# A planned attention and gated-convolution kernel: another plan for the same work, and the causal mask issued per head

## The chip, the cores and the metric

The kernel runs on one core of a Trainium2 chip. The metric is the device time of one execution in microseconds (us); lower is better. The inputs lie in HBM as float32, and the output goes back there as float32.

## The reference

```python
# q, k, v: [8, 8, 576, 64]   s: [8, 8, 576]   (batch, head, position, head width)
scores = q @ k.T / 8
cum    = cumsum(max(s, 0))                       # along the positions
scores = where(causal, -1e9, scores + min(-(cum_i - cum_j), 0))
attn   = softmax(scores)                         # [576, 576] per head
x      = (attn @ v) laid out as [8, 576, 512]    # heads side by side
# 5-tap causal convolution along the positions, per channel
gate   = sigmoid(sum_k conv_w[k] * shift(x, 4 - k))
out    = (gate * (x @ w_val)) @ w_out            # [8, 576, 512]
```

## The kernel before, in words

The eight batches are worked one after another, but heavily overlapped. Each batch has four head pairs; a head pair is numbered `n` = 4 x batch + pair, so `n` runs from 0 to 31. The decay `exp(cum)` is folded into v, so that a score needs only a plain `exp`. The steps of a head pair, with their lines in the profile:

- **Load and cast.** SyncE (SP) hands all transfers to its DMA queue. Q and K of a batch come in float32 and are cast to bf16 (L524; the last 64 positions, the "tail", L695 for batch 0 and L721 after it). For batch 0 this is cut into eight pieces (`first`, two per head pair) that DVE, ACT or POOL casts; from batch 1 on, POOL casts it in two large pieces.
- **Transpose.** TensorE (PE) transposes them into PSUM (`qk_T` L563, `tail_T` L552), ACT or DVE copies that to SBUF (`qk_evac` L567, `tail_evac` L555).
- **Scores.** `scores` (L572) has three steps of 1,024 columns (two heads x 512) in a pair of PSUM banks each; `exps` (L598, always on ACT) writes `P`. The diagonal blocks of both heads all lie in step 0, and POOL's `mask` (L604) zeroes what lies above the diagonal, over 2 x 512 columns, with one `affine_select`. The last 64 queries go the same way in `scores4`, `exp4` (L584) and `mask4` (L609), once per batch (in batch 0 per head pair).
- **Weighted sum.** `vprime` (L534, POOL; two of batch 0 on DVE) scales v; `av` (L619) multiplies P with it, `recip` (L624) and `norm` (L629) on DVE divide by the sum, `x_T` (L637) transposes back, `x_evac` (L641, DVE or ACT) copies to SBUF.
- **Gate.** Four `tap` steps per head pair, each on DVE (one instruction, L653 or for tap 1 L655) or on POOL (two instructions: L650 `tmp`, L651 `gp`); each tap reads the result of the tap before. Then `tanh` on ACT (L659).
- **Output.** `val` (L666) and `glu` (L672, DVE) per channel block, `outp` (L678), `out_evac` (L683, ACT or DVE), `store` (L686, SP).

The order of all this is no hand-written list. The program records every step as a task with an engine, an assumed duration, a due time, what it depends on and which buffers and PSUM banks it takes. `Plan.run` then plays these tasks through in a model and emits them in the order in which the model started them; each engine works through its own list strictly in that order. The due times are in the dictionary `DUE`, the choice of engine of the steps that have one is in `CHOICE` (a digit per step), `STAY` is the reluctance to turn PE between two kinds of work (scores, which use 64 rows of the array, and all the rest), and `BEHIND` is how far the DMA queue may be behind in the model before SP has to wait. All these are numbers fixed before the build; on the chip only the order and the engines are left of them.

```python
t = add("ACT", 0.905, n + 0.3 * i, lambda n=n, i=i: exps(n, i), [t], give=[("pair", ("s", n, i))])
es += [t] if i else [add("POOL", 0.75, n + due("mask"), lambda n=n: mask(n), [t])]
```

Of the kernel before, what the change touches and what calls it, by code (L numbers as in the profile page):

```python
# [14 lines left out]
ALU = mybir.AluOpType  # L15
# [190 lines left out]
def pcol(kb, qb):  # L206
    if kb == qb:
        return kb * 128
    if qb == 4:
# [13 lines left out]

DUE = dict(w=-179.07, lwv=6.9, lwo=25.99, cwv=119.71, cwo=21.81, av=-67.91, norm=-106.36, xt=-83.29,
           xe=-39.43, tap=73.53, dtap=-12.21, tanh=-21.14, val=7.28, dval=1.38, out=12.56, dout=0.92,
           oute=44.7, qt=-5.37, qe=224.11, tt=0.85, te=-141.54, s4=-66.86, vp=-112.81, cast=107.85,
           lqk=56.02, mask=-117.33, lv=13.25, av_e=68.91, av_l=-46.36, cast_e=-153.69, cast_l=-53.98,
           dout_e=-12.2, dout_l=-66.84, dtap_e=-10.04, dtap_l=-64.5, dval_e=14.84, dval_l=-0.73,  # L230
           lqk_e=-53.46, lqk_l=16.33, lv_e=84.68, lv_l=-81.16, mask_e=2.46, mask_l=30.46, norm_e=62.66,
           norm_l=45.33, out_e=82.66, out_l=-73.32, oute_e=83.06, oute_l=-53.09, qe_e=-68.49, qe_l=46.96,
           qt_e=-24.08, qt_l=3.94, s4_e=27.55, s4_l=-86.7, tanh_e=20.1, tanh_l=94.17, tap_e=-15.62,
           tap_l=-2.33, te_e=-55.59, te_l=-34.48, tt_e=-48.5, tt_l=-36.85, val_e=-96.42, val_l=2.31,
           vp_e=-46.58, vp_l=160.49, xe_e=32.24, xe_l=-1.61, xt_e=14.3, xt_l=-78.88, sd=-18.85, lcw=-44.05,
           cvt=23.68, rat=-67.55, lt0=-98.57, tailc0=29.75, lq0=-12.67, lq0d=2.97, cast0=-5.61,
           cast0d=127.18, lv0=-3.45, lv0d=2.76, vp0=32.35, vp0d=-5.83, tt0=62.96, te0=134.74, qt0=19.06,
           qe0=-26.31, q0d=25.23)


def due_of(b, name):
# [2 lines left out]

STAY = (1.35, 151.9)

BEHIND = 11.48

CHOICE = dict(tailc="2",
              vp0="1100",
              cast="00112001",
              wts="00",
              te="00000100",
              qe="01110110001000001001110000100100",
              xe="01111000001011110000000100100111",
              tap="00000000100001000000000100010000010000001100000000000010100000001000011000000010000100010000010010000110000100000100010010110000",
              oute="0010011001000000110010100000000010001100")


class Plan:
# [12 lines left out]
    def add(self, eng, us, key, emit, deps=(), take=(), give=(), mode="N", pick=None):  # L275
        alts = list(zip(eng, us)) if pick else [(eng, us)]
        eng, us = alts[int(CHOICE[pick[0]][pick[1]]) if pick else 0]
        if pick:
            emit = partial(emit, eng)
        t = dict(pick=pick, alts=alts, eng=eng, us=us, key=key, emit=emit, deps=[d for d in deps if d is not None], take=take,  # L280
                 give=give, mode=mode, n=len(self.tasks), done=None)
        self.tasks.append(t)
        return t
# [101 lines left out]
def main_path(ctx, tc, q, k, v, s, moe_w_val, moe_conv_w, moe_w_out, out, okcnt):  # L385
# [5 lines left out]
    nc = tc.nc  # L391
# [4 lines left out]
    add, slot = plan.add, plan.slot  # L396
# [49 lines left out]
    w = one.tile([128, NKB, 64], FP32, name="w")  # L446
# [29 lines left out]

    t = add("DVE", 0.65, DUE["sd"], relu, [t_s])
    t = add("DVE", 1.3, DUE["sd"], total, [t])
    t = add("DVE", 0.75, DUE["sd"], centre, [t])
    t = add("PE", 1.2, DUE["w"], decay_T, [t], take=[("bank", "w")])  # L480
# [5 lines left out]
    for m, (nm, src, dst, sc) in enumerate((("wv", moe_w_val, wv, 1.0), ("wo", moe_w_out, wo, 0.5))):  # L486
# [3 lines left out]
        t = add("SP", 2.8, DUE["l" + nm], load, take=[("qkf", nm)])  # L490
# [9 lines left out]
    t = add("SP", 0.3, DUE["lcw"], lambda: nc.sync.dma_start(out=cw, in_=moe_conv_w))  # L500
    t = add("PE", 0.3, DUE["cvt"], conv_T, [t], take=[("bank", "cw")])
# [97 lines left out]
                             func=AF.Exp, scale=0.125)  # L599


    def mask(n):
        d = slot["Pt", n][:, :, 0:512].rearrange("k h (g q) -> k h g q", g=4)
        nc.gpsimd.affine_select(out=d, in_=d, pattern=[[0, 2], [0, 4], [1, 128]], compare_op=ALU.is_ge, fill=0.0, base=0,  # L604
                                channel_multiplier=-1)

    def mask4(b, ps_):
# [80 lines left out]
    for b in range(B):  # L688
        n0 = 4 * b
        due = partial(due_of, b)  # L690
        old = lambda name: [T.get((name, b - 2, i)) for i in range(4)]

        if b == 0:
# [3 lines left out]
            for p in range(4):  # L697
                for wh in range(2):
# [3 lines left out]
                    t = add("SP", 0.82, DUE["lq0"] + DUE["lq0d"] * p + wh * 0.01, ld)  # L702
                    T["cast", 0, wh, p] = add(("DVE", "ACT", "POOL"), (0.32, 0.5, 0.8), DUE["cast0"] + p * DUE["cast0d"], lambda e, p=p, wh=wh: cast_qk(
                        copy[e], 0, wh, HP[p], slot["f", 0, wh, p]), [t], pick=("cast", 2 * p + wh))
                t = add("SP", 1.45, DUE["lv0"] + DUE["lv0d"] * p, lambda p=p: load_v_pair(p))
                T["vp", 0, p] = add(("DVE", "POOL"), (0.85, 1.25), DUE["vp0"] + p * DUE["vp0d"], lambda e, p=p: vprime(
                    nc.vector if e == "DVE" else nc.gpsimd, 0, p), [t, t_w], pick=("vp0", p))
        else:
            fs = []
            for wh in range(2):  # L710
# [3 lines left out]
                t = add("SP", 3.25, n0 + due("lqk"), ld, take=[("qkf", (b, wh))])  # L714
# [5 lines left out]
            t = add("SP", 1.45, n0 + due("lqk") + 0.5, lambda b=b: load_tail(b), [T.get(("tailc", b - 2))])  # L720
# [4 lines left out]
            for p in range(4):  # L725
# [4 lines left out]
        t = T["tt", b] = add("PE", 0.25, n0 + due("tt") if b else DUE["tt0"], lambda b=b: tail_T(b), [t_tail] + old_s,  # L730
                             take=[("bank", ("tt", b))])
        t_te = add(("ACT", "DVE"), (0.49, 0.6), n0 + due("te") if b else DUE["te0"], lambda e, b=b: tail_evac(e, b), [t],
                   give=[("bank", ("tt", b))], pick=("te", b))
        for p in range(4):
            t = T["qt", b, p] = add("PE", 0.45, n0 + p + due("qt") if b else DUE["qt0"] + p * DUE["q0d"], lambda b=b, p=p: qk_T(b, p),
                                    [T["cast", b, 0, p], T["cast", b, 1, p]] + old_s, take=[("bank", ("qt", b, p))])
# [4 lines left out]
        for ps_ in ([[p] for p in range(4)] if b == 0 else [[0, 1, 2, 3]]):  # L741
            n = len(ps_)
            t = T["s4", b, ps_[-1]] = add(
                "PE", 0.06 + 0.035 * n, n0 + ps_[0] + due("s4"), lambda b=b, ps_=ps_: scores4(b, ps_),
                [t_te] + [T["qe", b, p] for p in ps_] + [T.get(("av", b - 2, p)) for p in range(4)],
                take=[("pair", ("s4", b, ps_[0]))], mode="R")
            t = add("ACT", 0.08 + 0.1 * n, n0 + ps_[0] + due("s4"), lambda b=b, ps_=ps_: exp4(b, ps_), [t],
                    give=[("pair", ("s4", b, ps_[0]))])
            t = add("POOL", 0.15 + 0.11 * n, n0 + ps_[0] + due("mask"), lambda b=b, ps_=ps_: mask4(b, ps_), [t])
            for p in ps_:  # L750
                e4[p] = t
        for p in range(4):
            n = n0 + p
            es = []
            for i in range(3):
                take = [("pair", ("s", n, i))] + ([("P", n)] if i == 0 else [])
                t = T["s", n, i] = add("PE", 0.26, n + 0.3 * i, lambda n=n, i=i: scores(n, i),
                                       [T["qe", b, p], t_te if i else None, T.get(("s", n, i - 1)), T.get(("s", n - 1, 2))],
                                       take=take, mode="R")
                t = add("ACT", 0.905, n + 0.3 * i, lambda n=n, i=i: exps(n, i), [t], give=[("pair", ("s", n, i))])  # L760
                es += [t] if i else [add("POOL", 0.75, n + due("mask"), lambda n=n: mask(n), [t])]
            for hh in range(2):
                t = T["av", b, p] = add("PE", 0.45, n + due("av") + 0.1 * hh, lambda n=n, hh=hh: av(n, hh),
                                        [t] if hh else es + [e4[p], T["vp", b, p], T.get(("xt", n - 8))],
                                        take=[] if hh else [("pair", ("av", n))], give=[("P", n)] if hh else [])
            t = add("DVE", 0.13, n + due("norm"), lambda n=n: recip(n), [t])
            t = T["norm", n] = add("DVE", 0.74, n + due("norm"), lambda n=n: norm(n), [t], give=[("pair", ("av", n))])
            t = T["xt", n] = add("PE", 0.3, n + due("xt"), lambda n=n: x_T(n),
                                 [t] + [T.get(("val", n0 - 8 + c, hf)) for c in range(4) for hf in range(2)]
                                 + [T.get(("tap1", n - 8))], take=[("bank", ("x", n)), ("gp", n)])  # L770
            t = T["xe", n] = add(("DVE", "ACT"), (0.37, 0.65), n + due("xe"), lambda e, n=n: x_evac(e, n), [t],
                                 pick=("xe", n))
            for sh in range(1, 5):
                t = add(("DVE", "POOL"), (0.73, 2.25), n + due("tap") + sh * due("dtap"), lambda e, n=n, sh=sh: tap(e, n, sh),
                        [t, t_cw], give=[("bank", ("x", n))] if sh == 4 else [], pick=("tap", 4 * n + sh - 1))
                if sh == 1:
                    T["tap1", n] = t
            T["th", n] = [add("ACT", 0.59, n + due("tanh"), lambda n=n: tanh(n), [t], take=[("th", n)],
                              give=[("gp", n)])]

        for c in range(4):
            n = n0 + c
# [8 lines left out]
        for i in range(NKB):  # L791
# [4 lines left out]
            t = add(("ACT", "DVE"), (0.49, 0.6), n0 + due("oute") + due("dout") * i, lambda e, b=b, i=i: out_evac(e, b, i),  # L796
                    [t], take=[("ot", (b, i))], give=[("bank", ("o", b, i))], pick=("oute", 5 * b + i))
# [82 lines left out]
```

## Time and profile before

| what | value |
|---|---|
| median of 3 runs | 216.9 us (216.85 to 217.32) |
| the profiled execution, its own time | 216.85 us |
| its span in the profile | 215.1 us |
| busy: PE, DVE, ACT, POOL | 176.6, 172.8, 166.0, 177.0 us |
| time with which the chain of waits charges POOL | 31% of the span |
| granted TensorE clock, mean | 0.965 |

The span runs from the first to the last recorded event of the core; the 1.75 us between it and the execution's time lie around it. "Busy" is the summed time of an engine's instructions. All four computing engines are within 11 us of each other, so a share of the whole span doesn't say which of them holds the others up: that has to be read stretch by stretch.

### The profile page before, as it was taken

The numbers are of one execution on the slowest core, as the hardware profiler recorded it, in microseconds if no ns is written. First come the engines' busy times: TensorE is split into PE (matmuls) and PEld (weight loads), VectorE is DVE, ScalarE is ACT, GpSimd is POOL, SyncE is SP. The second block draws the span as 40 slices with busy tenths as digits, with TensorE's granted clock in tenths as the row PEclk, the third lists the DMA queues.
The fourth block names the chain that finished last, engine by engine and source line by source line (L and its number), as shares of the span: only waits on it lengthen the run. The fifth ranks groups of instructions, "written<-read, shape, count | busy, mean of one in ns | idle before, by whom it ended". The sixth has DMA issues, their size and how long they took to land.

```text
span 215.1 us, 5995 instructions
## 1 busy us (share of the span) xinstructions
PE 176.6 (82%) x2394; PEld 120.2 (56%) x2411; DVE 172.8 (80%) x295; ACT 166.0 (77%) x214; POOL 177.0 (82%) x161
## 2 busy tenths in 40 slices
PE   0488866788997997699998898789996998998980
PEld 0355755357655756367745674657664665664630
DVE  0496798696999895788989898899979687889930
ACT  2579269967798789979899999588996899965430
POOL 5069576799989999999999999999996899985400
PEclk9999979699999999979999999999999799999998
DMA  4998999999999599928994911186057122114333
GB/s 103 318 215 253 388 187 255 334 229 283 204 364 334 172 222 369 370 91 160 306 392 159 213 28 50 52 169 150 0 126 199 38 83 78 49 52 168 129 122 113
DMA packets 69230, 40.48 MB, mean 188 GB/s; under 512 B 47109, under 2 KB 63493, under 8 KB 69194
## 3 DMA queue, kind: packets, MB, share of 16 engines
q1 hardware_dynamic: 69194, 40.01, 67.8%
q8 instruction: 21, 0.34, 0.7%
q14 instruction: 15, 0.12, 0.2%
HBM read 30.57 MB, written 9.44 MB: 186 GB/s over the span
## 4 chain that ended last, share of the span: by engine, by line
POOL 31%; PE 20%; DVE 13%; issue 13%; ACT 12%; SPq 4%; DMA 3%; POOLq 0%; DVEq 0%; ACTq 0%
POOL Vp L534 8%; POOL gp L651 7%; POOL tmp L650 7%; ACT P L598 6%; PE banks L619 6%; PE banks L678 5%; PE banks L666 5%; POOL P L604 5%; DVE gp L653 3%; DVE xn L629 3%; DMA first<-in_k_dram 2%; DVE glu L672 2%; PE banks L572 2%; PE banks L563 2%; SPq L540 2%
## 5 line engine op out<-in xcount | busy, mean ns | idle before, releaser
L598 ACT ACTIVATE P<-banks 128x1024 bf16<-128x1024 f32 x96 | 95.1, 1037 | 10.1 <-PE banks L572 9.6
L653 DVE SCALAR_TENSOR_TENSOR gp<-banks,ratio,gp 128x572 f32<-128x572 bf16 (+2 forms) x77 | 61.3, 804 | 6.2 <-POOL gp L651 5.5
L572 PE MATMUL banks<-QKT 64*128 64x128 bf16 (+4 forms) x576 | 39.1, 251 | 10.4 <-ACT P L598 4.2
L619 PE MATMUL banks<-Vp,P 128*128 128x65 bf16 x960 | 37.9, 200 | 5.9 <-POOL P L604 2.8
L666 PE MATMUL banks<-xT,wv 128*128 128x288 bf16 x256 | 40.5, 296 | 1.9 <-DVE gp L653 1.2
L619 PEld LDWEIGHTS <-P 128*128 128x128 bf16 x960 | 35.7, 102 | 11.4 <-issue 3.7
L678 PE MATMUL banks<-wo,glu 128*128 128x512 bf16 x143 | 38.4, 380 | 3.0 <-DVE glu L672 0.9
L534 POOL TENSOR_TENSOR Vp<-vst,w 128x650 bf16<-128x650 f32 x30 | 39.0, 1321 | 1.8 <-ACT w L481 1.8
L604 POOL TENSOR_SCALAR_AFFINE_SELECT P<-P 128x1024 bf16<-128x1024 bf16 x32 | 35.1, 1099 | 5.1 <-ACT P L598 4.8
L572 PEld LDWEIGHTS <-QKT 64*128 64x128 bf16 x576 | 18.9, 97 | 27.2 <-issue 20.1
L650 POOL TENSOR_TENSOR tmp<-xT,ratio 128x574 f32<-128x574 bf16 (+3 forms) x25 | 28.6, 1146 | 2.8 <-ACT xT L641 2.2
L666 PEld LDWEIGHTS <-wv 128*128 128x128 bf16 x256 | 23.3, 100 | 13.3 <-issue 6.8
L672 DVE SCALAR_TENSOR_TENSOR glu<-th,banks 128x288 bf16<-128x288 f32 x64 | 27.7, 446 | 3.1 <-PE banks L666 2.8
L651 POOL TENSOR_TENSOR gp<-tmp,gp 128x574 f32<-128x574 f32 (+2 forms) x19 | 26.8, 1413 | 3.7 <-DVE gp L653 2.4
L659 ACT ACTIVATE th<-gp,halfw 128x576 f32<-128x576 f32 x32 | 24.9, 785 | 5.3 <-DVE gp L653 5.3
L629 DVE TENSOR_TENSOR xn<-banks,recs 128x640 bf16<-128x640 f32 x32 | 26.2, 820 | 0.5
L683 ACT COPY ot<-banks 128x512 f32<-128x512 f32 (+1 forms) x29 | 17.1, 599 | 9.7 <-PE banks L678 7.2
L678 PEld LDWEIGHTS <-glu 128*128 128x128 bf16 x160 | 14.3, 98 | 17.2 <-issue 4.7
L567 ACT COPY QKT<-banks 128x1024 bf16<-128x1024 bf16 x20 | 20.0, 1024 | 4.8 <-PE banks L563 4.8
L655 DVE SCALAR_TENSOR_TENSOR gp<-xT,ratio,banks 128x576 f32<-128x576 bf16 x26 | 21.0, 808 | 0.8 <-ACT xT L641 0.3
L637 PE MATMUL banks<-ident,xn 128*128 128x128 bf16 x160 | 14.1, 219 | 3.2 <-DVE xn L629 2.0
L567 DVE COPY QKT<-banks 128x1024 bf16<-128x1024 bf16 x12 | 14.4, 1216 | 2.6 <-PE banks L563 2.6
(63 smaller groups left out, 176.3 us busy)
## 6 DMA issues: line engine op xcount, KB each, us to landing
out_dram<-ot SPq DMA_DIRECT2D x32, 256.0 KB, 2.9
qkf<-in_q_dram SPq DMA_DIRECT2D x7, 1024.0 KB, 7.3
qkf<-in_k_dram SPq DMA_DIRECT2D x7, 1024.0 KB, 8.5
vst<-in_v_dram SPq DMA_DIRECT2D x28, 256.0 KB, 4.8
vst<-in_v_dram SPq DMA_DIRECT2D x15, 128.0 KB, 5.0
tail<-in_q_dram SPq DMA_DIRECT2D x8, 128.0 KB, 7.9
tail<-in_k_dram SPq DMA_DIRECT2D x8, 128.0 KB, 7.0
first<-in_q_dram SPq DMA_DIRECT2D x4, 256.0 KB, 4.7
```

Of the source, the lines that this page charges most:

```text
L534: eng.tensor_tensor(Vps[b % 2][:, :, h], vst[:, :, h], w[:, :, b * 8 + 2 * p:b * 8 + 2 * p + 2].unsqueeze(3).to_broadcast([128, NKB, 2, 65 ...
L567: copy[e](QKTs[b % 2][:, :, p, 0:512].rearrange("d w (x j) -> d w x j", j=4), slot["qt", b, p].rearrange("d w (j x) -> d w x j", j=4))
L572: nc.tensor.matmul(ps[:, hh, c0:c0 + nq], QKTs[b % 2][r, 1, p, k0:k0 + 128], QKTs[b % 2][r, 0, p, q0:q0 + nq], **kw)
L598: nc.scalar.activation(out=slot["Pt", n][:, :, step * 512:(step + 1) * 512], in_=slot["s", n, step], func=AF.Exp, scale=0.125)
L604: nc.gpsimd.affine_select(out=d, in_=d, pattern=[[0, 2], [0, 4], [1, 128]], compare_op=ALU.is_ge, fill=0.0, base=0, channel_multiplier=-1)
L619: nc.tensor.matmul(ps[:, hh, qb * 65:qb * 65 + 65], lhsT, Vps[b % 2][:, kb, 2 * p + hh, :], start=(kb == 0), stop=(kb == qb))
L629: nc.vector.tensor_tensor(xns[b % 2][:, :, p * 128:(p + 1) * 128].rearrange("t g (h d) -> t h g d", h=2), pv[:, :, :, 0:64], recs[:, n].un ...
L650: nc.gpsimd.tensor_tensor(tmp[:, o:S], xs[:, 2 - sh + o:2 - sh + S], r.to_broadcast([128, S - o]), ALU.mult)
L651: nc.gpsimd.tensor_tensor(gp[:, o:S], tmp[:, o:S], gp[:, o:S] if o else xs[:, 2:], ALU.add)
L653: nc.vector.scalar_tensor_tensor(gp[:, o:S], slot["x", n][:, 0:S - o], r, gp[:, o:S], ALU.mult, ALU.add)
L666: nc.tensor.matmul(ps, wv[:, dc, c * 128:(c + 1) * 128], xTs[b % 2][:, dc, 2 + o:290 + o], start=(dc == 0), stop=(dc == 3))
L678: nc.tensor.matmul(ps, glus[b % 2][:, c, WIN[i]:WIN[i] + 128], wo[:, c, :], start=(c == 0), stop=(c == 3))
```

## The change

The tasks, their buffers and their arithmetic stay; the numbers of the plan are others, and one task is cut in two.

- `mask` is issued once per head (two `affine_select` of 512 columns) in place of once per head pair (one of 1,024). The plan now counts 2 x 0.6 us for it, before 0.75 us.
- `DUE`, `STAY` (1.35, 151.9 to 2.87, 127.12) and `BEHIND` (11.48 to 10.11) have other values, which puts the tasks of every engine in another order.
- `CHOICE` moves steps between engines. Counted over all batches, before to after: taps on POOL 25 to 19 (tap 1: 6 to 4; tap 2: 8 to 3; tap 3: 5 to 2; tap 4: 6 to 10); `qk_evac` on DVE 12 to 11; `x_evac` on DVE 18 to 19; `out_evac` on DVE 11 to 9; `tail_evac` on DVE 1 to 0; casts of batch 0 on DVE, ACT, POOL 4, 3, 1 to 3, 4, 1; the tail cast of batch 0 from POOL to DVE.

The built order, read from the two programs: PE turns between scores and other work 116 times before and 106 times after; a tap follows a tap of the same head pair on the other engine (DVE and POOL) 30 times before and 20 after. In the first batch SP hands out s one pair of pieces earlier, and the first two v transfers before the last Q and K pieces:

```
SP before: tail, conv_w, q0 k0, q1 k1, s, q2 k2, q3 k3, v0, v1, v2, v3, batch 1 ...
SP after:  tail, conv_w, q0 k0, s, q1 k1, q2, v0, k2, v1, q3 k3, v2, v3, batch 1 ...
ACT before: tail_evac 0, cast q1, qk_evac 0, cast k1, exp4 0, exps 0 (three), cast k3, w, exp4 1, ...
ACT after:  tail_evac 0, cast k0, cast q1, cast q2, exp4 0, exps 0 (three), w, exp4 1, ...
DVE before: conv ratios, cast q0, cast k0, relu, cumsum, cast k2, centre, qk_evac 1, qk_evac 2, cast q3, ...
DVE after:  tail cast, conv ratios, cast q0, relu, qk_evac 0, cumsum, centre, qk_evac 1, cast k2, cast q3, qk_evac 2, ...
PE end before: ... x_T 31, outp 6 (two), val 28, outp 6 (three), count, val 29, 31, 30, outp 7 (five)
PE end after:  ... x_T 31, outp 6 (five), val 28, 29, count, val 31, 30, outp 7 (five)
```

In the last batch POOL has the taps 30/1, 30/3 and 30/4 before, 30/1 and 30/2 after.

```diff
-           ... sd=-18.85, lcw=-44.05,
-           cvt=23.68, rat=-67.55, lt0=-98.57, tailc0=29.75, lq0=-12.67, lq0d=2.97, cast0=-5.61,
-           cast0d=127.18, lv0=-3.45, lv0d=2.76, vp0=32.35, vp0d=-5.83, tt0=62.96, te0=134.74, qt0=19.06,
-           qe0=-26.31, q0d=25.23)
+           ... sd=-15.74, lcw=-22.57,
+           cvt=-10.73, rat=-74.99, lt0=-86.14, tailc0=47.9, lq0=-10.92, lq0d=2.77, cast0=12.28,
+           cast0d=98.87, lv0=-5.37, lv0d=1.44, vp0=70.86, vp0d=-8.38, tt0=49.65, te0=84.67, qt0=29.8,
+           qe0=0.26, q0d=39.82)
...
-STAY = (1.35, 151.9)
-BEHIND = 11.48
+STAY = (2.87, 127.12)
+BEHIND = 10.11
...
-CHOICE = dict(tailc="2",
+CHOICE = dict(tailc="0",
               vp0="1100",
-              cast="00112001",
+              cast="01121001",
               wts="00",
-              te="00000100",
-              qe="01110110001000001001110000100100",
-              xe="01111000001011110000000100100111",
-              tap="00000000100001000000000100010000010000001100000000000010100000001000011000000010000100010000010010000110000100000100010010110000",
-              oute="0010011001000000110010100000000010001100")
+              te="00000000",
+              qe="11100110000000001110110000100000",
+              xe="01111000001010110000000010110011",
+              tap="00010000100000000001000100010000000100000000100000000000100000000001000000000101000000100000000100010000000001100001000011000000",
+              oute="0000001000001000010101100000010000001100")
...
-    def mask(n):
-        d = slot["Pt", n][:, :, 0:512].rearrange("k h (g q) -> k h g q", g=4)
-        nc.gpsimd.affine_select(out=d, in_=d, pattern=[[0, 2], [0, 4], [1, 128]], compare_op=ALU.is_ge, fill=0.0, base=0,
+    def mask(n, hh):
+        d = slot["Pt", n][:, hh, 0:512].rearrange("k (g q) -> k g q", g=4)
+        nc.gpsimd.affine_select(out=d, in_=d, pattern=[[0, 4], [1, 128]], compare_op=ALU.is_ge, fill=0.0, base=0,
                                 channel_multiplier=-1)
...
-                es += [t] if i else [add("POOL", 0.75, n + due("mask"), lambda n=n: mask(n), [t])]
+                es += [t] if i else [add("POOL", 0.6, n + due("mask") + 0.01 * hh, lambda n=n, hh=hh: mask(n, hh), [t])
+                                     for hh in range(2)]
```

All other entries of `DUE` (due times of the later batches) change as well.

More of the change, by code (lines that the diff above doesn't have):

```diff
@@ L222 @@
 NEG = -30000.0
[L226 to L235, printed above, removed]
-           cvt=23.68, rat=-67.55, lt0=-98.57, tailc0=29.75, lq0=-12.67, lq0d=2.97, cast0=-5.61,
-           cast0d=127.18, lv0=-3.45, lv0d=2.76, vp0=32.35, vp0d=-5.83, tt0=62.96, te0=134.74, qt0=19.06,
-           qe0=-26.31, q0d=25.23)
@@ new lines @@
+DUE = dict(w=-146.29, lwv=18.35, lwo=25.55, cwv=66.29, cwo=20.07, av=-62.19, norm=-66.39, xt=-62.08,
+           xe=-40.28, tap=59.48, dtap=-11.23, tanh=-60.59, val=7.98, dval=1.19, out=13.07, dout=0.7,
+           oute=35.59, qt=-4.95, qe=212.03, tt=1.64, te=-107.11, s4=-34.19, vp=-83.31, cast=103.59,
+           lqk=30.41, mask=-106.85, lv=19.28, av_e=59.94, av_l=-18.88, cast_e=-150.32, cast_l=-44.48,
+           dout_e=-18.55, dout_l=-90.65, dtap_e=-17.77, dtap_l=-16.53, dval_e=23.29, dval_l=2.97,
+           lqk_e=-22.85, lqk_l=14.05, lv_e=56.66, lv_l=-121.96, mask_e=19.74, mask_l=17.23, norm_e=50.91,
+           norm_l=8.42, out_e=93.56, out_l=-44.02, oute_e=121.54, oute_l=-99.96, qe_e=-63.7, qe_l=55.19,
+           qt_e=-69.75, qt_l=4.1, s4_e=-5.62, s4_l=-62.13, tanh_e=26.16, tanh_l=103.46, tap_e=-8.19,
+           tap_l=19.63, te_e=-35.56, te_l=-17.97, tt_e=-12.58, tt_l=-2.26, val_e=-88.07, val_l=-6.49,
+           vp_e=-38.23, vp_l=139.1, xe_e=-4.6, xe_l=10.49, xt_e=-36.76, xt_l=-24.73, sd=-15.74, lcw=-22.57,
+           cvt=-10.73, rat=-74.99, lt0=-86.14, tailc0=47.9, lq0=-10.92, lq0d=2.77, cast0=12.28,
+           cast0d=98.87, lv0=-5.37, lv0d=1.44, vp0=70.86, vp0d=-8.38, tt0=49.65, te0=84.67, qt0=29.8,
+           qe0=0.26, q0d=39.82)
```

## The prediction, made before the changed kernel ran

> **What bounds the kernel now.** I began with the top of the page, whose busy times hardly tell the engines apart, so I read the slices next, then the chain of waits.
>
> ```profile
> span 215.1 us, 5995 instructions
> PE 176.6 (82%) x2394; PEld 120.2 (56%) x2411; DVE 172.8 (80%) x295; ACT 166.0 (77%) x214; POOL 177.0 (82%) x161
> ...
> POOL 5069576799989999999999999999996899985400
> ...
> POOL 31%; PE 20%; DVE 13%; issue 13%; ACT 12%; SPq 4%; DMA 3%; POOLq 0%; DVEq 0%; ACTq 0%
> ```
>
> POOL is idle early and late and solid from about the eighth slice on; the chain charges it most, and DMA 3%. The view by windows says where (columns: length, then busy us of PE, PEld, DVE, ACT, POOL with instruction counts, the clock, the DMA share, GB/s):
>
> ```profile
> 0.00:40.00 40.00, 24.84 (x333) 18.61 (x334) 27.67 (x43) 25.93 (x36) 24.12 (x35) 0.95 0.94 248
> 40.00:145.00 105.00, 92.90 (x1350) 63.86 (x1358) 90.39 (x158) 90.83 (x114) 102.72 (x85) 0.97 0.82 224
> 145.00:180.00 35.00, 31.51 (x441) 21.02 (x445) 30.82 (x54) 30.78 (x40) 31.50 (x27) 0.95 0.38 97
> 180.00:195.00 15.00, 14.39 (x205) 9.80 (x205) 12.71 (x25) 11.85 (x17) 14.08 (x13) 1.00 0.19 72
> 195.00:215.10 20.10, 13.00 (x76) 6.87 (x73) 11.20 (x21) 6.58 (x11) 4.55 (x4) 0.97 0.38 129
> ```
>
> From 40 to 145 us POOL works 102.72 of 105 us (98%) and the others 86 to 88%: there POOL is the bound. From 145 to 180 it stands at 90%, like PE; after 180 PE leads (14.39 of 15), and after 195 POOL has almost nothing. So what POOL saves counts fully between 40 and 145, in part up to 195, and hardly elsewhere.
>
> **POOL, the mask in two.** The timeline of POOL gives the price from start to start, which is what a full queue pays (columns: start, busy, engine, line):
>
> ```profile
> 112.23 0.66 POOL L609 TENSOR_SCALAR_AFFINE_SELECT P<-P 128x512 bf16<-128x512 bf16 x1
> 112.86 2.52 POOL L534 TENSOR_TENSOR Vp<-vst,w 128x650 bf16<-128x650 f32 x2
> 115.34 1.10 POOL L604 TENSOR_SCALAR_AFFINE_SELECT P<-P 128x1024 bf16<-128x1024 bf16 x1
> 116.40 1.28 POOL L534 TENSOR_TENSOR Vp<-vst,w 128x650 bf16<-128x650 f32 x1
> ```
>
> A select of 1,024 columns keeps the queue for 116.40 - 115.34 = 1.06 us, one of 512 (`mask4`, the size of the new half) for 0.63. Two halves cost 1.26, so the split adds about 0.2 us per head pair, 32 x 0.2 = 6.4 us in all. Lower end: if a half cost just half of 1.06, nothing is added; upper end by busy times, 2 x 0.66 - 1.10 = 0.22, 7.0 us. I take 6.4, since the 512-column row has the very size. No gain is in it: the data is the same.
>
> [...]
>
> **POOL, the taps.** The groups:
>
> ```profile
> L650 POOL TENSOR_TENSOR tmp<-xT,ratio 128x574 f32<-128x574 bf16 (+3 forms) x25 | 28.6, 1146 | 2.8 <-ACT xT L641 2.2
> L651 POOL TENSOR_TENSOR gp<-tmp,gp 128x574 f32<-128x574 f32 (+2 forms) x19 | 26.8, 1413 | 3.7 <-DVE gp L653 2.4
> L653 DVE SCALAR_TENSOR_TENSOR gp<-banks,ratio,gp 128x572 f32<-128x572 bf16 (+2 forms) x77 | 61.3, 804 | 6.2 <-POOL gp L651 5.5
> ```
>
> A tap on POOL is 1.15 + 1.41 = 2.56 us (a tap 1, whose second instruction is a shape of its own at 1.20, is 2.35), on DVE 0.80. 25 to 19: two tap 1 (4.7) and four others net (10.2) leave, -14.9 us on POOL. The tail cast of batch 0 leaves too (0.6). POOL's sum: 177.0 - 14.9 - 0.6 + 6.4 = 167.9 us.
>
> Where these fall, by the built order of POOL:
> - From the mask of head pair 5 (starts at 42.72) to that of 23 (145.17), the stretch in which POOL is the bound: 18 masks cost 18 x 0.2 = 3.6 more, one `mask4` moves out (-0.63), taps go from 11 to 9 (-2.35 - 2.56 = -4.9). Net **-1.9 us**, nearly all on the path. Bounds: -5.5 (halves that add nothing) to -1.6 (by 0.22).
> - From 23 to 31 (187.61): masks +1.6, `mask4` +0.63, taps 8 to 6, -4.9: net -2.7 us. PE and POOL share this stretch, so half passes: **-1.3** (0 to -2.7).
> - Behind mask 31: 4 taps to 2, -5.1 us, beside PE, which sets the end; **0** here.
> - Ahead of mask 5 the sums are equal within 0.3 us.
>
> **DVE and ACT.** DVE: taps +6 x 0.80 = 4.8; one `qk_evac` less, -1.2; `x_evac` +0.45; two `out_evac`, -1.4; tail copy -0.4; one cast -0.6; the tail cast +0.5: +2.2 us, 172.8 to 175.0. ACT: +1.0 - 0.65 + 2 x 0.6 + 0.6 + 0.6 = +2.8, 166.0 to 168.8. In 40:145 DVE has 14.6 us free and ACT 14.2, so these are covered; without that cover they would cost up to 2.8 us. PE's instructions are the same.
>
> **Waits between engines.** 30 to 20 changes of engine within a chain of taps, where DVE waited 5.5 us for POOL in seven places (L653's row); DVE isn't the bound there, so 0, with -1.5 as the far end. PE turns 116 to 106 times:
>
> ```profile
> PEld L572 <- issue: 20.1, 52, 1.1
> ```
>
> The weight load of the scores stands idle 0.39 us at 52 of the turns. Ten fewer are 3.9 us of PE, which PE at 88% needn't pass on: 0, with -3.9 as the far end. The order of SP's transfers: the same bytes and issues; in the 40:145 window the chain is on POOL, not on a landing, so 0; what goes late first is the v load, which waits for the last `vprime` of the batch before, and that comes no later.
>
> **The start.** `qk_evac 0` moves from ACT to DVE, behind `relu`, which waits for s. Before, s went out at 4.89 and relu began at 10.01, 5.1 us later. It now goes out two issues (0.5 us each) earlier, so relu starts near 9.0, the copy (1.22 us) ends near 10.7 where ACT's ended at 10.10; `cast q2` (landed at 10.64) now also stands in front of ACT's first exp. First exp +0.6 us. Against that ACT stood idle 3.27 + 0.78 us at 21.7 to 26.1 for the scores of head pair 3, whose `qk_evac` now is on ACT, behind `cast k3` and `x_evac 1`. Between -1 and +1; I take **+0.3**.
>
> **The end.** Behind norm 31, DVE gets a tap and a glu more and an `out_evac` less (0.80 + 0.45 - 0.68 = +0.57), but no longer waits for POOL's taps 30/3 and 30/4 (there 0.28 and 0.43 us). PE runs all of batch 6's output ahead of `val 28`. -1 to +1; **0**.
>
> **Sum.** -1.9 - 1.3 + 0.3 = -2.9 us at full passing. I let four fifths of POOL's 3.2 pass, because the next engines are at 88% and each waits for others: -2.6 + 0.3 = -2.3. The profiled execution took 216.85 us (span 215.1 and 1.75 around it; the median of the runs is 216.9, the same to 0.05): 216.85 - 2.3 = **214.5 us**.
>
> **Rivals.**
> 1. *Nothing passes.* POOL's 1.9 us turn into waits for PE, DVE and ACT, which are all within 12% of full in the same window. For it: the four sums become 176.6, 175.0, 168.8 and 167.9, and PE's is unchanged. Against it: no engine but POOL gets over 88.5% in 40:145. Time 216.5 to 217.3.
> 2. *Slower: the last tap on POOL blocks ACT.* Tap 4 goes from 6 to 10 on POOL, and tap 4 is what `tanh` waits for; ACT works in order, so a late tap 4 holds the exps queued behind `tanh`, with them the scores' PSUM banks, PE and then POOL's own masks. A tap 4 on POOL is 2.56 - 0.80 = 1.76 us longer. All ten exposed: 17.6 us. It decides above 2.6 / 10 = 0.26 us each; with a third exposed (0.6 us each) it is 6 us, less 2.3: 220.5 us. Against it: with six such taps before, ACT's waits name DVE alone,
>
> ```profile
> ACT th L659 <- DVE gp L653: 5.3, 6, 2.1
> ```
>
> and in the new order two to six exps stand between the mask ahead of the tap and the `tanh`. For it: tap 0/4 now stands ahead of the tail cast of batch 1 and has just two. A milder form gives 217.5 to 219.
> 3. *Much faster.* PE was the second bound throughout, and the ten turns (3.9 us) come on top: 216.85 - 2.3 - 3.9 = 210.7 us.
> 4. *The transfers matter after all*, as the name of the change says. Waits for a DMA outside the first 12 us are small (POOL's tail casts, 1.1 us in two), so it gives 215.5 to 217 and joins rival 1.
>
> **How the numbers follow.** A difference below 0.2% (0.4 us) can't be told from none here. Forecast, 212 to 216.4: 0.50. Much faster: 0.08. Nothing passes: 0.10, of which 0.07 lies within 0.2% and the rest on both sides. Slower by the tap or another wait of a new order: 0.32. Faster 0.59, same 0.07, slower 0.34. Range 211.2 to 219.5: below it lies about half of the "much faster", above it a quarter of the slower cases. The forecast's own range is 212 to 216.4.
>
> **What would show it.** In the changed profile: 64 selects at L604 at about 0.66 us; POOL near 168 us busy; masks 5 to 23 in about 100 us in place of 102.45; POOL still the busiest engine in that stretch. Wrong if the halves cost 0.55 or less (then POOL gains 6 us more), if ACT waits over 5 us for `gp` of POOL at `tanh` (rival 2), if the first exp comes over 1 us later and mask 5 with it, or if POOL falls under 93% between masks 5 and 23 with no gain (rival 1).

## The result, and the profile after

The changed kernel takes 211.51 us in the median (211.02 to 211.99, 4 runs) against 217.0 us before: ratio 0.9745, 95% interval 0.9716 to 0.9774, so about 5.5 us faster. It was measured twice more beside the kernel before: 0.9737 (0.9684 to 0.9791) and 0.9736 (0.9695 to 0.9776). The profiled execution took 211.99 us, its span is 210.3 us, 4.8 us less than before. The forecast was 2.3 us: the right way, less than half of the size.

The top of the page after, POOL's slices and the chain of waits:

```profile
span 210.3 us, 6022 instructions
PE 173.6 (83%) x2390; PEld 119.9 (57%) x2411; DVE 173.8 (83%) x298; ACT 168.7 (80%) x218; POOL 165.2 (79%) x180
...
POOL 4059589579999999999999999997979969838000
...
PE 30%; DVE 25%; POOL 14%; ACT 12%; issue 10%; DMA 3%; SPq 2%; ACTq 0%; DVEq 0%; POOLq 0%
```

POOL has 11.8 us less to do and is charged with 14% of the chain in place of 31%; PE and DVE now carry it. The stretches, cut at the masks of head pairs 5, 23 and 31 and at the end of the last `norm`, show where the time came from. First before, then after (columns: stretch, length, busy us of PE, PEld, DVE, ACT, POOL with counts, clock, DMA share, GB/s):

```profile
0.00:42.72 42.72, 27.16 (x345) 19.90 (x346) 28.87 (x44) 28.65 (x40) 26.76 (x37) 0.92 0.95 256
42.72:145.17 102.45, 90.62 (x1340) 62.62 (x1348) 89.36 (x155) 88.28 (x112) 100.08 (x83) 0.98 0.82 220
145.17:187.61 42.44, 38.73 (x545) 25.66 (x551) 36.60 (x64) 37.78 (x48) 39.03 (x33) 0.96 0.34 92
187.61:194.25 6.64, 6.36 (x94) 4.59 (x92) 6.01 (x12) 4.60 (x7) 5.88 (x6) 1.00 0.17 61
194.25:215.10 20.85, 13.75 (x81) 7.38 (x80) 11.95 (x23) 6.66 (x11) 5.22 (x5) 0.97 0.38 131
```

```profile
0.00:43.53 43.53, 27.71 (x359) 20.99 (x360) 30.65 (x50) 29.01 (x40) 25.99 (x41) 0.96 0.96 252
43.53:141.96 98.43, 87.68 (x1333) 61.91 (x1343) 86.55 (x149) 89.37 (x112) 96.92 (x96) 0.97 0.84 226
141.96:184.39 42.43, 40.05 (x543) 26.12 (x551) 40.09 (x73) 39.36 (x52) 36.03 (x39) 1.00 0.34 98
184.39:188.56 4.17, 4.12 (x78) 3.38 (x78) 4.00 (x8) 4.10 (x6) 1.23 (x2) 1.00 0.32 118
188.56:210.30 21.74, 14.01 (x82) 7.54 (x82) 12.54 (x24) 6.86 (x11) 5.04 (x4) 0.93 0.35 120
```

The start costs 0.8 us more, the stretch from mask 5 to mask 23 gives 4.0, the next one nothing, the rest 1.6 (6.64 + 20.85 - 4.17 - 21.74). In the third stretch the length is the same, but PE does 1.3 and DVE 3.5 us more in it: work that then is missing behind mask 31. The granted clock is no explanation: its mean is 0.965 before and 0.969 after, and in the stretch that gave most it is 0.98 before and 0.97 after.

The price of the mask in two, in POOL's timeline of the changed kernel:

```profile
63.69 1.24 POOL L604 TENSOR_SCALAR_AFFINE_SELECT P<-P 128x512 bf16<-128x512 bf16 x2
64.89 1.15 POOL L650 TENSOR_TENSOR tmp<-xT,ratio 128x572 f32<-128x572 bf16 x1
```

A pair of halves keeps the queue 64.89 - 63.69 = 1.20 us, 0.14 more than the single select's 1.06; the prediction had taken 0.2 from the `mask4` row.

### The profile page after: what moved, and what is told of

Same layout as the page of the kernel before. It is cut to its first block, busy times and chain, and to the rows that moved or that the text cites. A ratio compares the mean times of both kernels' runs of the same rounds, so it can differ in the third digit from the quotient of the medians.

```text
span 210.3 us, 6022 instructions
## 1 busy us (share of the span) xinstructions
PE 173.6 (83%) x2390; PEld 119.9 (57%) x2411; DVE 173.8 (83%) x298; ACT 168.7 (80%) x218; POOL 165.2 (79%) x180
## 4 chain that ended last, share of the span: by engine, by line
PE 30%; DVE 25%; POOL 14%; ACT 12%; issue 10%; DMA 3%; SPq 2%; ACTq 0%; DVEq 0%; POOLq 0%
DVE gp L653 8%; PE banks L666 8%; PE banks L678 6%; PE banks L619 6%; PE banks L572 5%; ACT P L598 5%; DVE glu L672 4%; POOL gp L651 4%; DVE xn L629 3%; POOL Vp L534 3%; DMA first<-in_q_dram 3%; POOL tmp L650 3%; DVE gp L655 3%; PE banks L563 3%; POOL P L604 2%
## 5 line engine op out<-in xcount | busy, mean ns | idle before, releaser
L653 DVE SCALAR_TENSOR_TENSOR gp<-banks,ratio,gp 128x574 f32<-128x574 bf16 (+2 forms) x81 | 64.5, 806 | 1.0 <-POOL gp L651 0.3
L604 POOL TENSOR_SCALAR_AFFINE_SELECT P<-P 128x512 bf16<-128x512 bf16 x64 | 39.2, 636 | 8.3 <-ACT P L598 8.2
L619 PEld LDWEIGHTS <-P 128*128 128x128 bf16 x960 | 34.4, 100 | 7.3 <-issue 3.2
L619 PE MATMUL banks<-Vp,P 128*128 128x65 bf16 x960 | 36.3, 197 | 2.5 <-ACT P L598 2.3
L572 PEld LDWEIGHTS <-QKT 64*128 64x128 bf16 x576 | 19.2, 97 | 32.2 <-issue 23.6
L683 ACT COPY ot<-banks 128x512 f32<-128x512 f32 (+1 forms) x31 | 18.4, 598 | 9.9 <-PE banks L678 9.3
L655 DVE SCALAR_TENSOR_TENSOR gp<-xT,ratio,banks 128x576 f32<-128x576 bf16 x28 | 22.4, 802 | 2.7 <-ACT xT L641 2.0
L650 POOL TENSOR_TENSOR tmp<-xT,ratio 128x572 f32<-128x572 bf16 (+3 forms) x19 | 21.9, 1151 | 3.2 <-ACT xT L641 3.0
L651 POOL TENSOR_TENSOR gp<-tmp,gp 128x572 f32<-128x572 f32 (+2 forms) x15 | 22.3, 1485 | 2.4 <-DVE gp L653 1.3
L563 PE MATMUL banks<-ident,qb 128*128 128x128 bf16 x128 | 13.8, 236 | 2.2 <-DVE qb L524 0.8
L567 DVE COPY QKT<-banks 128x1024 bf16<-128x1024 bf16 x11 | 13.2, 1214 | 2.5 <-PE banks L563 2.5
```

The source lines that it names most:

```text
L567: copy[e](QKTs[b % 2][:, :, p, 0:512].rearrange("d w (x j) -> d w x j", j=4), slot["qt", b, p].rearrange("d w (j x) -> d w x j", j=4))
L572: nc.tensor.matmul(ps[:, hh, c0:c0 + nq], QKTs[b % 2][r, 1, p, k0:k0 + 128], QKTs[b % 2][r, 0, p, q0:q0 + nq], **kw)
L604: nc.gpsimd.affine_select(out=d, in_=d, pattern=[[0, 4], [1, 128]], compare_op=ALU.is_ge, fill=0.0, base=0, channel_multiplier=-1)
L619: nc.tensor.matmul(ps[:, hh, qb * 65:qb * 65 + 65], lhsT, Vps[b % 2][:, kb, 2 * p + hh, :], start=(kb == 0), stop=(kb == qb))
L651: nc.gpsimd.tensor_tensor(gp[:, o:S], tmp[:, o:S], gp[:, o:S] if o else xs[:, 2:], ALU.add)
L653: nc.vector.scalar_tensor_tensor(gp[:, o:S], slot["x", n][:, 0:S - o], r, gp[:, o:S], ALU.mult, ALU.add)
```

## The experiments

Two theories were held against each other. **Load**: POOL's work in the stretch between masks 5 and 23 sets the time. **Order**: the new order of the engines' lists gains by itself. In most of these kernels the steps are recorded in exactly the order of the one or the other plan, and only what is issued for a step is changed ("in place"), because a plan made anew is another kernel altogether, as the two planned runs below show.

### The mask in the old order, and undone in the new one

```diff
 # e1: kernel before, in mask(n)                     # e2: changed kernel, in mask(n, hh)
+for hh in range(2):                                  +if hh == 0:
+    affine_select(slot["Pt", n][:, hh, 0:512])       +    return
-affine_select(slot["Pt", n][:, :, 0:512])            +affine_select(slot["Pt", n][:, :, 0:512])
```

> The kernel before with its own order; only at each mask two selects of 512 columns are issued in place of one of 1,024. Theory L (POOL's load sets the time between masks 5 and 23): a pair of halves keeps the queue 2 x 0.595 = 1.19 us in the changed kernel's trace against 1.05, so POOL gets 0.14 x 32 = 4.5 us more, of which 18 x 0.14 = 2.5 lie in the bound stretch; time 217 + 2.5 to 3.5 = 219.5 to 220.5. Theory F (finer masks let av of the first head start earlier, and that is the gain): below 216. Theory O (the new order of the engines' lists is the gain, the load is incidental): 216.5 to 218.

Measured: 220.11 us, ratio 1.0159 (1.0106 to 1.0213). The stretch of 102.45 us becomes 105.1. The split alone costs 3 us, as load says. (The four runs, with granted clocks from 0.930 to 0.982, all lie between 219.6 and 220.8 us, so the clock isn't the reason.)

> The changed kernel with its own order; at each head pair one select of 1,024 columns is issued where its second half stood, the first half is left out of the queue. Theory L: POOL, at 98% in the bound stretch of the changed kernel too, gets 18 x 0.14 = 2.5 us free there; time 211.5 - 2 to 2.5 = 209 to 209.5. Theory F: slower than 211.5 by 1 us or more. Theory O: 211 to 212.

Measured: 210.5 us, ratio 0.9737 (0.9673 to 0.9802), not separable there from the changed kernel. So the two were put side by side, five rounds each:

> The changed kernel's order with one select per head pair, again, beside the changed kernel on the same chip in the same rounds. Theory L for the new order (POOL's 2 us less between masks 5 and 23 pass): 1 us below the changed kernel, 210.3 to 210.8. Theory C (the other lists take it back by the end): within 0.4 us of it.

> The changed kernel as it is, for the comparison in the same rounds: 211.3 to 211.9.

Measured: 210.13 us, ratio 0.9662 (0.9626 to 0.9697), beside 211.91 us, 0.9736 (0.9695 to 0.9776). One select is about 1.8 us better in the new order as well; the intervals just touch. The mask's split is a loss in both orders, more sharply shown in the old one, and the version with one select is the fastest measured here. The stretch from mask 5 to mask 23, first in this run, then in e2:

```profile
41.60:139.35 97.75, 88.13 (x1343) 61.76 (x1342) 85.97 (x148) 88.82 (x112) 94.66 (x77) 0.97 0.85 231
42.30:138.70 96.40, 86.53 (x1340) 60.93 (x1340) 85.95 (x147) 88.77 (x112) 94.45 (x77) 0.98 0.87 232
```

The three profiles of the changed kernel have 98.43, 98.60 and 98.63 us there. So the bound stretch falls by 0.7 to 2.2 us, for 18 x 0.14 = 2.5 us less on POOL. The rest of the gain lies ahead of it: mask 5 comes 1.2 to 2.2 us sooner, of which the five masks before it account for 0.7; the remainder has no cause shown here.

### More load in the new order

```diff
+for _ in range(2 if hh and 5 <= n < 23 else 1):      # in mask(n, hh): the second half twice
     nc.gpsimd.affine_select(...)
```

> The changed kernel with its own order; for head pairs 5 to 22 the second half of the mask is issued twice (the second time changes nothing in P): 18 x 0.595 = 10.7 us more on POOL in the bound stretch, nothing elsewhere. Theory L (POOL still sets that stretch in the changed kernel, 98.5% busy): 211.5 + 9 to 10.7 = 220.5 to 222. If the changed kernel had come free of POOL: 211.5 to 215.

Measured: 222.66 us, ratio 1.0261 (1.0220 to 1.0302): about 11 us above the changed kernel's 211.5 to 211.9, for 10.7 us of load. Its stretch from mask 5 to mask 23:

```profile
42.57:152.54 109.97, 92.58 (x1361) 64.07 (x1362) 88.65 (x152) 91.21 (x113) 108.03 (x114) 0.95 0.79 210
```

It was 98.43 us. POOL added is time added; POOL is still a bound of the changed kernel.

### Less load in the old order

```diff
 def tap(e, n, sh):
+    if (n, sh) in [(13, 3), (19, 3)]:                # e4: (8,2) (10,2) (13,3) (17,2) (17,3) (19,3)
+        e = "DVE"                                    # e5: (29,2) (30,3) (30,4)
```

> The kernel before with its own order; taps 13/3 and 19/3 (both in the bound stretch) are issued on DVE (one instruction of 0.80 us) where they stood for POOL (2.6 us from start to start). Theory L: 5.2 us off POOL there, time 217 - 4 to 5 = 212 to 213. Theory O: 216 to 217.5, the load being incidental. My recorded sum (four fifths pass): 217 - 4.1 = 212.9.

Measured: 217.08 us, ratio 1.0034 (1.0000 to 1.0069): nothing.

> As the last one with six taps (8/2, 10/2, 13/3, 17/2, 17/3, 19/3) on DVE: 15.5 us off POOL, 4.8 us onto DVE, all between masks 5 and 23. Theory L with the other engines at 88% as the next limit: the stretch of 102.45 us can fall to what DVE (89.4 + 4.8 = 94.2) or PE (90.6) needs at 95 to 97%, about 97 us; time 210.5 to 212. If load alone counted: 217 - 15.5 = 201.5. Theory O: 215 to 218.

Measured: 216.58 us, ratio 0.9991 (0.9965 to 1.0016): nothing, with 15.5 us off an engine that was 98% busy (by busy time 14.7: 100.08 to 85.42). The profiled execution, 215.46 us, is the fastest of eleven. Its stretch and the chain of the whole span:

```profile
42.30:144.00 101.70, 90.42 (x1350) 62.47 (x1348) 92.95 (x162) 88.42 (x112) 85.42 (x71) 1.00 0.84 228
```

```profile
DVE 32%; PE 27%; ACT 17%; issue 8%; DMA 4%; POOL 4%; SPq 4%; DVEq 0%; ACTq 0%
```

POOL is out of the chain (4%), DVE is in its place, and the stretch is 0.75 us shorter. Load as I had stated it is refuted for the old order.

> The kernel before with its own order; only taps 29/2, 30/3 and 30/4, which stand at the end of POOL's list, are issued on DVE. Theory T (in the kernel before, DVE's in-order list waits for these taps at 187.9, 191.4 and behind norm 30, which puts norm 31 and the end later): norm 31 comes 1 to 2 us sooner after mask 31, and the time is 215 to 216. Rival (PE sets the end, as my prediction had it): 216.7 to 217.3; and if three more taps on DVE (2.4 us) count there, up to 219.

Measured: 217.39 us, ratio 0.9995 (0.9968 to 1.0021). `norm` 31 starts at 193.57, 5.9 us behind mask 31, much as in the kernel before (193.43 and 5.8). The taps at the end of POOL's list were no cause of the late end.

### What holds the old order when POOL doesn't

To see who took the gain, taps are left out (that part of the convolution is missing in the output): the six POOL taps of e4, six DVE taps of the same stretch, and both.

```diff
+    if (n, sh) in [(8, 2), (10, 2), (13, 3), (17, 2), (17, 3), (19, 3)]:   # e12; e13: (7,2) (9,2) (11,2)
+        return                                                             # (12,3) (15,2) (18,3); e14: all 12
```

> The kernel before, its own order; the six POOL taps 8/2, 10/2, 13/3, 17/2, 17/3, 19/3 are left out (that part of the convolution is missing): 15.5 us off POOL between masks 5 and 23, and nothing put on DVE instead. Theory D (in the run that moved them, DVE's 4.8 us more ate the gain): 209 to 212. Theory C (POOL, DVE, PE and ACT are bound together by the old order, POOL's 98% is only one of several full lists): 214.5 to 217.

Measured: 213.97 us, ratio 0.9837 (0.9773 to 0.9901). The stretch:

```profile
43.50:142.80 99.30, 89.75 (x1342) 61.86 (x1349) 89.15 (x155) 87.76 (x112) 85.29 (x71) 1.00 0.85 230
```

> The kernel before, its own order; six DVE taps in the same stretch (7/2, 9/2, 11/2, 12/3, 15/2, 18/3) are left out, 4.8 us off DVE, POOL as it was. Theory L (POOL alone bound): 216.5 to 217.5. Theory C: 215 to 217.

Measured: 216.91 us, ratio 0.9997 (0.9979 to 1.0015).

> Both sets of six taps left out. Theory C with POOL and DVE as the two lists bound together: 209 to 213, more than the two single effects added. If PE's and ACT's lists hold the old order by themselves: 214.5 to 216.5.

Measured: 213.32 us, ratio 0.9841 (0.9802 to 0.9881). Its stretches (masks 5, 23, 31, end), its chain, and two of the waits in the first of these stretches (columns of a wait: us in total, times, longest):

```profile
43.10:141.70 98.60, 89.36 (x1342) 61.92 (x1350) 85.31 (x149) 87.89 (x112) 85.45 (x71) 1.00 0.85 228
141.70:184.20 42.50, 37.46 (x545) 24.55 (x550) 36.16 (x64) 37.62 (x48) 39.08 (x34) 1.00 0.32 87
184.20:211.60 27.40, 20.07 (x172) 11.93 (x170) 17.95 (x33) 11.21 (x18) 11.05 (x10) 0.98 0.33 115
```

```profile
PE 37%; ACT 26%; DVE 14%; issue 8%; DMA 5%; SPq 4%; POOL 4%; DVEq 0%; ACTq 0%
```

```profile
ACT P L598 <- PE banks L572: 5.1, 7, 1.6
PE banks L572 <- ACT P L598: 2.7, 5, 0.9
```

Three findings. POOL was the bound of the old order, but only by about 3 us (2.1 to 4.9 by the interval): 15.5 us off it, with nobody paying, give no more (e12). DVE is not a bound there (e13), yet it has no room for those taps: putting their 4.8 us (six times 0.80; DVE's busy time in the whole span rose by 3.6) on DVE costs nearly all of that gain (e4 against e12). And below that PE and ACT, which by the two waits hold each other up, carry the chain, and the stretch stays at 98.6 us with no engine over 91% busy (e14): leaving out work of DVE as well adds nothing.

### Order and engines apart

```diff
-            emit = partial(emit, eng)                                          # e9: order before, engines
+            emit = partial(emit, alts[int(ISSUED[pick[0]][pick[1]])][0])       # and halves after; e10: reverse
```

> The order in which the steps are recorded is that of the kernel before; every step is issued on the engine that the changed kernel gives it (taps, copies, casts), and the mask in two halves. So the load of each engine is that of the changed kernel, the order the old one. Theory L (load): 211 to 213. Theory O (order): 216.5 to 220, since taking six taps off POOL gave nothing and the halves cost 3.

Measured: 229.18 us, ratio 1.0597 (1.0519 to 1.0674).

> The reverse: the steps in the order of the changed kernel, each on the engine that the kernel before gives it, and one select per head pair. POOL has its 25 taps again. Theory O (the order is what gained): 209.5 to 213. Theory L: 216 to 218. If order and engines only fit as a pair (a step stands where its own engine was free): over 218 here and in the run before.

Measured: 237.39 us, ratio 1.0907 (1.0855 to 1.0960). Both are far slower than either kernel, as only the third expectation (order and engines fit as a pair) had it. The waits, of e9 first and then of e10:

```profile
POOL P L616 <- ACT P L609: 16.1, 11, 4.0
```

```profile
DVE gp L666 <- POOL gp L664: 23.5, 11, 4.2
ACT th L672 <- DVE gp L666: 17.8, 11, 5.1
```

A step stands in its list where its own engine was free in the plan. On another engine it is in the way there, and all behind it wait; that is how these waits are read here, and no run tests it step by step. What the two runs do show is that neither load nor order gains alone: an order fits its own engines.

### Scores earlier in the old order

```diff
+    for key in [(6, 0), (10, 2), (13, 2)]:           # behind plan.run(): as early as inputs and banks allow
+        ...
+        plan.order.insert(to, plan.order.pop(place))
```

> The kernel before; in PE's list the scores 6/0, 10/2 and 13/2, around which ACT waited for PE by 1.59, 1.29 and 1.41 us, are put as early as their inputs and banks allow, ahead of val 0/0 to 2/1, of av 9 with val 7 and x_T 8, and of av 12 with val 8/0. Theory S (the old order brings scores late, ACT starves, and that is the bound next to POOL): 214 to 216. Rival (what is put behind them is then late for DVE by as much): 216.5 to 219.

Measured: 220.79 us, ratio 1.0164 (1.0135 to 1.0194), slower than both expectations. In the stretch DVE now waits for what was put behind:

```profile
DVE glu L672 <- PE banks L666: 6.1, 5, 3.2
```

In the kernel before, this wait is 2.8 us between 42 and 150 us. ACT's own wait for scores there is 8.9 us, against 7.4 before. Repairing single waits of an order by hand made new ones.

### The parts as written, with a plan made anew

```diff
 # e7: kernel before                                  # e8: changed kernel
-es += [add("POOL", 0.75, ..., mask(n))]              -es += [add("POOL", 0.6, ..., mask(n, hh)) x 2]
+es += [add("POOL", 0.6, ..., mask(n, hh)) x 2]       +es += [add("POOL", 0.75, ..., mask(n))]
```

> One part of the change alone, as written: the kernel before, its numbers of the plan, but the mask as two tasks of 0.6 us, and the plan made anew with that. Every list changes a little, POOL keeps its 25 taps. Theory L: as the halves in the old order, 219 to 221. Theory O (an order made with the right duration is the gain): 211 to 215.

Measured: 236.6 us, ratio 1.0896 (1.0845 to 1.0948).

> One part of the change undone, as written: the changed kernel with the mask as one task of 0.75 us and the plan made anew. POOL keeps 19 taps and has 32 selects of 1,024. Theory L: about as the single select in the new order, 208.5 to 211. Theory O (the order fits the split only): 213 or more.

Measured: 222.65 us, ratio 1.0247 (1.0214 to 1.0281). The first lies outside both expectations; the second lies where order had it, 9.65 us beyond the bound named. The same select in the same kernel takes 210 us when the order is kept (e2) and 222.65 when one assumed duration lets the plan order itself anew: with another duration beside them the same due times give a far slower order, and the spread between plans is several times what the change moved.

### A version meant to beat both

> A version meant to beat both: the changed kernel's order with one select per head pair, and taps 11/1 and 19/2 issued on DVE. In the new order one select brought the stretch from mask 5 to mask 23 from 98.4 to 96.4 us, so POOL's load passes there. Theory L for the new order: 5 us less on POOL, 1.6 more on DVE, 207 to 209.5. Theory C for the new order too: 210 to 211.5.

Measured: 210.78 us, ratio 0.9724 (0.9689 to 0.9759): faster than the kernel before, no better than one select alone. From mask 5 to mask 23 it takes 97.50 us, with 89.7 us of POOL's work in place of 94.7 (e16). In the new order, too, POOL's last 5 us are not worth more, once the taps must go to DVE.

> The changed kernel as it is, beside the others on one chip, so that they can be held against it: 211 to 212.

Measured: 211.84 us, ratio 0.9737 (0.9684 to 0.9791).

## Why the prediction was right in sign and wrong in size

The step that failed is the term for the stretch from mask 5 to mask 23, and with it the four fifths. The sum has -2.3 us, and the span fell by 4.8. That stretch gave 2.1 us more than its term, a fifth of POOL's 3.2 us was struck off without cause (0.6), the stretches behind it gave 0.3 more, and the start cost 0.5 more than forecast. The measured 211.51 us lie below the forecast's own range (212 to 216.4) and near rival 3's 210.7, but not for that rival's reason.

- **The stretch from mask 5 to mask 23, forecast -1.9, measured -4.0: the term that was mis-sized.** One part is the half of the mask: I took 0.63 us from start to start from the `mask4` row, it is 0.60, so the 18 split masks cost 2.5 us and not 3.6, and POOL's sum falls by 3.0 (in busy time 100.08 - 96.92 = 3.2). The rest, 4.02 - 3.16 = 0.86 us, is POOL's own idle time, 102.45 - 100.08 = 2.4 us before and 98.43 - 96.92 = 1.5 after: the new lists feed POOL better. I had set that to nothing.
- **Four fifths pass: wrong.** It took 0.64 us off the forecast. In the new order the stretch got shorter by more than POOL's saving. In the old order, though, nothing of such a saving passes when DVE takes the taps (e3, e4), and a fifth when nobody does (e12). The factor that I applied is no property of the loads; it belongs to the pair of order and load. The right sign was therefore in part luck. The saving was priced in the kernel before, where moving such work from POOL to DVE gains nothing, and the prediction gave no reason why the new lists would let it pass; two other plans for the same work took 222.65 and 236.6 us (e8, e7).
- **Mask 23 to 31, -1.3, and the end, 0: together -1.6 measured, in another place.** The third stretch kept its length. PE did 40.05 in place of 38.73 us in it and DVE 40.09 in place of 36.60, and the end got shorter by that. That PE sets the end fits the chain behind mask 31 (in the kernel before, `outp` and `val` on PE are 45% of it); that the end therefore stays was wrong, since PE can be given its work sooner. That this is what shortened it is read from these columns; no run moved it alone. The run without twelve taps shows the same from the other side: in the old order its last stretch still takes 27.4 us (before 6.64 + 20.85 = 27.5), against 25.9 in the new one.
- **The start, +0.3: +0.8 at mask 5.** ACT's first exps, counted without `exp4`, start at 12.00 in place of 10.85, 1.15 us later where 0.6 was forecast. Of the two reasons given, the copy behind `relu` did not delay them: it ended at 9.86, sooner than ACT's 10.10. The other, `cast q2` in front of them, shows. ACT waited 0.98 us for its transfer, which I had taken to land at 10.64, as before:

```profile
11.31 0.62 ACT L524 CAST qb<-first 128x512 bf16<-128x512 f32 x1 [0.98 <-DMA first<-in_q_dram]
12.00 2.84 ACT L598 ACTIVATE P<-banks 128x1024 bf16<-128x1024 f32 x3
```

- **DVE and ACT covered: the sums right** (173.8 and 168.7 us against forecast 175.0 and 168.8), the cover not shown. The chain charges DVE 25% after and 13% before, and in the old order DVE's extra taps did cost time (e4 against e12).
- **PE's turns, 0: right.** Ten turns fewer, and the weight load of the scores even waits longer, 23.6 us in place of 20.1, so rival 3's ten turns are not where the extra time came from:

```profile
PEld L572 <- issue: 23.6, 53, 1.7
```

- **Rival 2, the last tap in front of `tanh`: not seen.** ACT's wait of that kind is 1.6 us in three places:

```profile
ACT th L659 <- POOL gp L651: 1.6, 3, 0.9
```

- **The bound itself.** POOL at 98% beside others at 86 to 88% was read as one bound with room next to it. (Rival 1's "within 12% of full" holds for PE alone; DVE and ACT had 90.39 and 90.83 of 105 us.) More load on POOL did count in full (e1, e6); less load had about 3 us of room in the old order before PE and ACT (e12, e14), and none where DVE had to take it (e4). The Trainium skill (Perfetto Trace Analysis, Identifying the Most-Contended Engine) calls the busiest engine the one to relieve first. Here relieving it in place gave nothing where DVE took the work, and a fifth of it where nobody did. The same page (Optimizing Scalar/DVE Operations) warns that moving work between POOL and DVE may not help because they share a read port. The taps on DVE are not slowed in e4, though (804 ns mean before, 802 with six more), so no run shows the port as the cause. What is left is DVE's list, the place of the taps in it or its greater load; no run tells these two apart.

What stays open: which of the moved steps make the new order better. Order and engines could not be separated, and the one attempt to repair the old order by hand failed. That the new order gains more than its engines' sums of work explain is shown in one comparison: e14, with POOL at 162.3, DVE at 167.8 and ACT at 165.3 us, all lighter than in the changed kernel (165.2, 173.8, 168.7), and PE the same (173.8 against 173.6), still needs 213.32 us, and its interval (0.9802 to 0.9881) lies above the changed kernel's (at most 0.9791 in the three measurements).

## What to carry to other kernels

In this kernel an engine that was 98% busy in a stretch told that more load there would cost; it didn't tell that less load would pay, since the other engines work through fixed lists that were ordered around it. Leave the work out once, in place, to learn how much room there is before the next bound, and move it afterwards. In a planned kernel compare changes with the order held fixed, and judge a new plan only by its measured time.

## What the runs showed that was not expected

- One `affine_select` of two heads x 512 columns keeps POOL 1.06 us from start to start, two of 512 columns 1.20: the second instruction costs 0.14 us. In place that was 3 us of 217 in the old order and 1.8 us in the new one.
- One assumed duration of the plan (0.75 in place of two times 0.6) moved the same kernel from about 210 to 222.65 us.
